# Linear attention into a channel mix on one core: k in uneven runs of tokens into a ring of squares, r and v on token tiles, and a new order

## The chip, the core and the metric

The kernel runs on one core of a Trainium2 chip. The metric is device time in microseconds of one execution, the median of several. Its engines are TensorE (PE, whose weight loads are listed as PEld), VectorE (DVE), ScalarE (ACT), GpSimd (POOL) and SyncE (SP). SP, ACT and POOL also issue DMAs, each into a queue of its own; the loads that convert float32 to bfloat16 on the way are issued by POOL.

## The reference

Eight batches of eight heads, 576 tokens, head width 64: a linear attention whose output (512 wide per token) goes through a channel mix.

```python
def _attn_ref(q, k, v):                       # each (8, 8, 576, 64)
    q_s = softmax(q, axis=-1)                 # over the head width
    k_s = softmax(k, axis=2)                  # over the tokens
    kv = np.einsum('bhsd,bhse->bhde', k_s, v)
    return np.einsum('bhsd,bhde->bhse', q_s, kv)

def _moe_ref(x, mu_k, mu_r, w_k, w_v, w_r):   # x (8, 576, 512)
    x_prev = tokens shifted by one, zero first
    xk = mu_k * x + (1.0 - mu_k) * x_prev
    xr = mu_r * x + (1.0 - mu_r) * x_prev
    k = np.maximum(xk @ w_k, 0.0)             # 512 -> 1024
    v = k * k @ w_v                           # 1024 -> 512
    r = 1.0 / (1.0 + np.exp(-(xr @ w_r)))
    return r * v
```

## The kernel before

Everything is bfloat16 on TensorE with float32 sums in PSUM. Every piece of work is an operation with a short name; `graph` makes the operations with what each depends on, and the long string `ORDER` gives the one sequence in which they are emitted. An engine runs its operations in that sequence. A token of `ORDER` may change the engine of an operation (`ACT!load00q1`), give it a buffer (`:0`), or make it wait for another operation (`^rrec000`).

**Attention, per batch b and half g of the heads** (names end in b, g and for the first two batches a quarter index): `load` brings q, k and v; `expq`, `expk` are exps on ACT; `rsum`, `rrec`, `scale` (DVE) make the softmax of q; `cast` (ACT) makes v bfloat16 for batches from 1 on, while batch 0's v is converted by its load into `vb`. `T` are the transposes of q (L361), `KV` the products of k and v (L391), `Z` the sums over k; from batch 2 on all of this is one block, `B` or `TKV`. `rz`, `kvn` or `w` (DVE) divide by the sums, `qt` (ACT) copies the transposed q out of PSUM, `edge` copies the column for the shift.

**Mix.** Batches 0 and 1 are fused: `wp` multiplies the small matrix by mu and 1 - mu, and `X` (L479) makes xk (m=0) or xr (m=1) directly, in two pieces of 288 tokens; `x...` (L489, L492) copies them to `xk` and `xr`, the first piece on ACT, the second on DVE. From batch 2 on, `X` (L517) makes x, `xb`/`xs` copy it (ACT), and `diff`, `sc`, `mix` (DVE) mix it with the shifted tokens.

**Channel mix.** `xk` and `xr` hold a ring of four batches (2304 tokens). The ring is cut into units of 512, 512, 512, 512 and 256 tokens, twice. In each unit, `k` (L601) makes 8 slices of 128 features from 4 matmuls each; `relu` (L588, ACT) and `sq` (L592, DVE) write the squares into one of two buffers `k_a`, `k_b` (`k2s`); for each 128 tokens of the unit `r` (L633) and `th` (ACT), then `v` (L653, 8 matmuls), `o` (L659, DVE) and two stores `st` on SP. In the first two units the k matmuls are emitted in halves, first the feature tiles of g=0 and then those of g=1.

`fill` (L292) are matmuls on a constant tile that nothing reads; 18 of them are in this order, all before the first `X`. POOL issues, in this order, batch 0's v, then batch 1's first q half, the four parts of w_k and the rest of batch 1 with w_r and w_v between:

```python
ident load00v load01v load10q0 wk11 wk00 load10q1 wk01 wk10 load11v0 load11q0 load11q1 wr ...
```

PSUM has four single banks (`mm`) and two double ones (`att`); for batch 0 an allocation `any` may use either.

Of the kernel before, what the change touches and what calls it, by code (L numbers as in the profile page):

```python
# [41 lines left out]
ORDER = """
ACT!rows ident load01q0:0 load00q0:1 ACT!load00q1 load01q1 load00v consts ACT!load00k1:2 load00k0
ACT!load01k0:3 load01v zero late fill:3 warm load10q0:4 fill.2:2 fill.3:3 wk11 fill.4:2 fill.5:3
wk00 expq000:0 wide:0 load10q1 load01k1 rsum000:0 wk01 rrec000 expq011:1 scale000:0 wk10 expq010
fill.6^rrec000:3 rsum011:1 fill.7^expq011:2 expq001 fill.8^expq010:3 rsum010 fill.9^rsum011:2
fill.31:2 rsum001 fill.10^expq001:3 expk000:0 fill.11^rsum010:2 rrec010 widecopy scale010:1
fill.12^expk000:3 expk001 fill.13:2 fill.32:2 rrec011 rrec001 KV000:0 scale001 load11v0:5 KV001
scale011 T00:1 expk011:1 Z00 expk010 fill.14:3 rz00:0 kvn00:0 fill.16:3 rest KV011:2 load11q0:6
KV010 T01:0 qt00:0 wp000:0 edge00 wp001 Z01 load11q1 qt01:1 fill.17:3 rz01:1 kvn01:1 X000:1.3  # L50
expq100:2 wp010:1 wr edge01 X001:2.0 x0000 x0001 X010:1.3 x0010 load10v0:7 k02:0 wv0 x0100 x0101
k00:1 wp011 k03:2 x0011 k01:3 load10k1:8 k00.2 k01.2 relu00:0 k02.2 load11v1 relu01:1 X011:1.0
relu02:2 load10v1 sq01:0 k03.2 x0110 x0111 k05:1 load10k0 relu03:1 sq00 expq111:0 load11k0:9 k04:3
expq101 k06:0 expq110 rsum101:2 relu04:0 k07:2 sq03 sq02 relu06:1 rsum110:3 load11k1 r03:3
cast100:0 sq04 muload wv1 r00:0 relu07:2 cast110:1 sq07 r01:2 rsum111 relu05:0 th00:0 rrec101
r02:1 rsum100 th03:1 wv2 th01:2 v010:0 rrec100 rrec111 rrec110 sq05 expk101:2 load20v0:10
scale100:2 v030:3 th02:3 load20q0:0 scale101 cast111 v000:2 cast101 scale110:0 expk100 v020:1
scale111 expk110:0 load21q0:1 TKV10:0 expk111 load20k0:2 rz10:2 kvn10:0 TKV11:1 qt10:2 wp101:0
v021 rz11:0 load21v0:3 kvn11:1 v011 sq06 qt11:0 v031 wp100 load30v0:4 v001 edge10 v012 load30q0:6
edge11 v022 o01 cast200:2 X100:0.1 load21k0:5 wp110:1 v002 x1001 x1000 v032 o00 mu:0 load31q0:7  # L60
X110:1.0 o02 load40q0:8 k13:2 x1100 expq200:1 x1101 k11:1 wp111 expq210:2 rsum200:0 k13.2 k11.2
load31k0:9 X111:1.0 relu13:2 mucopy o03 load30k0:10 expk200:1 k12:0 x1111 st03 k14:2 rrec200 x1110
st00.2 rsum210:1 load41q0:0 st00 k10:3 relu11:0 X101:0.1 st01 relu14:1 sq11:1 st03.2 cast210:0
sq13 k10.2 load31v0:1 st02.2 x1011 k12.2 relu10:0 k15:1 x1010 sq10 load40v0:2 k16:2 scale200:1
relu12:2 relu15:0 k17:3 expq300:0 rrec210 sq14 r10:0 sq12 relu17:1 rsum300:2 TKV20:1 relu16:2
cast300:1 load40k0:3 r11:1 rrec300 rz20:1 scale210:2 th10:4 r13:3 expk210:2 r12:2 w20:0 sq16
qt20:1 scale300:0 v100:0 load50q0:6 th11:5 B21:0.1 sq15 expq310:1 sq17 v120:1 rz21:2 th13:6 w21:1
rsum310:3 xs20:0 xb20 v110:3 load41k0:4 v121 qt21:0 edge20 diff20:0 load50k0:5 v111 th12:0
sc2001:0 expq400:2 rrec310 X21:1.0 sc2000 o11 r20:2 load50v0:7 xb21:1 mix200 v130:3 o12 xs21
th20:1 load41v0:8 edge21 v101 st12 diff21:1 expk300:0 st01.2 v131 sc2100:1 sc2101 expk310:1  # L70
load51q0:10 sc2010:2 TKV30:1 mix210 cast310:2 o13 k20:1 load51v0:9 scale310:1 k21:2 relu20:2
cast400:0 o10 k25:3 rz30:0 load61q0:1 sc2011 st10 k23:1 relu21:0 w30:2 sc2111:0 st12.2 qt30:2
sq20:0 st10.2 k27:0 rsum400:0 expk400:2 k22:2 sq21 load51k0:2 mix201 relu23:1 B31:0.1 relu22:2
rrec400 sc2110 relu27:0 k24:1 sq22 load60q0:3 xs30:0 rz31:1 mix211 relu25:2 k26:2 xb30 sq27 sq25
r23:0 w31:0 relu24:0 edge30 scale400:2 qt31:1 r22:3 expq410:0 diff30:0 r21:1 sq23 B40:1.0 sc3001:1
th21:2 load60v0:0 rsum410:1 relu26:2 v200:1 xs31:1 xb31 sc3000 sq26 v220:2 sq24 th22:0 edge31
mix300 th23:4 v201 expq500:1 sc3011:2 diff31:1 v221 o20 cast410:1 load60k0:6 v210:3 sc3101:0 st20
o22 expk410:0 v230:0 st20.2 load70q0:8 sc3100 sc3010 v211 mix310 expq510:2 load61k0:4 mix301 v231
expk500:1 load61v0:10 o21 k30:1 o23 st21.2 cast500:2 load71q0:5 sc3110:1 k31:2 st02 sc3111 st23
rz40:2 mix311 relu30:1 load71k0:7 k32:3 st22 expk510:2 sq30:1 st11 rrec410 k33:0 w40:1 st22.2  # L80
scale410:0 relu31:2 st13.2 load71v0:2 k34:1 relu32:0 st21 relu33:1 sq31 k35:2 qt40:0 sq32 sq33
# [737 lines left out]
```

## Time and profile before

| what | value |
|---|---|
| runs | 201.43, 201.09, 199.63 us; median 201.09 |
| profiled execution | span 199.1 us from its first to its last instruction; no time beside the span is given for it |
| granted TensorE clock | 1.00 throughout |
| PE, PEld, DVE, ACT, POOL busy | 187.2, 92.3, 150.8, 145.7, 43.6 us |
| bytes | 33.56 MB read, 9.44 MB written, DMA queues busiest up to 100 us |
| first fused mix, first k, first r | 16.17, 18.65, 26.29 us |
| last matmul, end of the span | about 195.2, 199.1 us |

Busy time of an engine is the time in which at least one of its instructions ran. Pipelined matmuls overlap, so a 128x512 matmul is shown with 379 ns although the next begins 216 ns after it. A line of the timeline gives the start, the length, the engine, the source line and the tiles; the brackets give the engine's idle time just before and what ended it.

### The profile page before, as it was taken

What the parts mean: (1) busy time and instruction counts of PE and PEld (TensorE: products, weight loads), DVE (VectorE), ACT (ScalarE), POOL (GpSimd) and SP (SyncE); (2) the same over time, 40 slices, a digit from 0 to 9 for tenths busy, and PEclk for the clock granted to TensorE, in tenths of its full rate; (3) what the DMA queues carried; (4) which work ended last, traced back from release to release, by engine and by line L of the source; (5) the groups of instructions that cost most, each with busy time, mean ns of one, the idle gap of its engine ahead of it and who ended that gap; (6) DMA issues with size and microseconds to landing.
All of it is one profiled execution on the core that took longest, in us unless ns stands there. A gap on an engine that the chain in (4) does not pass through costs nothing.

```text
span 199.1 us, 5164 instructions
## 1 busy us (share of the span) xinstructions
PE 187.2 (94%) x2059; PEld 92.3 (46%) x2085; DVE 150.8 (76%) x348; ACT 145.7 (73%) x224; POOL 43.6 (22%) x70
## 2 busy tenths in 40 slices
PE   6598999989999999999999999999999999999992
PEld 2045445434444444445565545544444544444751
DVE  1588486889989999999999995999825459732531
ACT  3377798799999999999999488777624762552340
POOL 8435438954424312622000000000000000000000
PEclk9999999999999999999999999999999999999999
DMA  6999999999999998799942130422044013402513
GB/s 199 256 276 281 279 336 230 367 397 393 415 393 395 400 407 328 243 412 405 376 116 54 45 90 0 102 63 54 3 105 107 0 23 85 105 2 53 121 40 105
DMA packets 16544, 40.13 MB, mean 202 GB/s; under 512 B 2300, under 2 KB 5640, under 8 KB 16520
## 3 DMA queue, kind: packets, MB, share of 16 engines
q0 software_dynamic: 9440, 27.99, 42.3%
q1 hardware_dynamic: 6400, 10.65, 19.5%
q10 hardware_dynamic: 680, 1.15, 1.6%
q8 instruction: 16, 0.26, 0.6%
q14 instruction: 8, 0.07, 0.1%
HBM read 33.56 MB, written 9.44 MB: 216 GB/s over the span
## 4 chain that ended last, share of the span: by engine, by line
PE 50%; issue 1%; ACT 0%; DVE 0%
PE mm_c L653 7%; PE mm_d L653 6%; PE mm_d L601 5%; PE mm_c L601 4%; PE mm_a L653 4%; PE mm_b L601 4%; PE mm_a L601 4%; PE mm_b L633 3%; PE mm_b L653 3%; PE mm_a L633 3%; PE mm_d L633 2%; PE mm_c L633 1%; PE att_b L517 1%; PE att_a L517 1%; PE att_a L391 1%
## 5 line engine op out<-in xcount | busy, mean ns | idle before, releaser
L653 PEld LDWEIGHTS <-k_a 128*128 128x128 bf16 x144 | 13.8, 98 | 16.9 <-DVE k_a L592 0.6
L633 PEld LDWEIGHTS <-xr 128*128 128x128 bf16 x144 | 13.9, 98 | 16.4 <-issue 0.2
L653 PEld LDWEIGHTS <-k_b 128*128 128x128 bf16 x152 | 14.3, 98 | 15.0 <-issue 0.6
L633 PE MATMUL mm_b<-wr,xr 128*128 128x512 bf16 x45 | 12.2, 379 | 0.2
L601 PEld LDWEIGHTS <-wk_bb 128*128 128x128 bf16 x80 | 7.8, 98 | 7.7
L601 PEld LDWEIGHTS <-wk_ba 128*128 128x128 bf16 x80 | 7.7, 98 | 7.8 <-issue 0.3
L601 PEld LDWEIGHTS <-wk_ab 128*128 128x128 bf16 x80 | 7.6, 98 | 8.0 <-DVE xk L489 0.5
L601 PEld LDWEIGHTS <-wk_aa 128*128 128x128 bf16 x80 | 7.4, 98 | 8.3 <-issue 1.0
L633 PE MATMUL mm_a<-wr,xr 128*128 128x512 bf16 x39 | 10.2, 379 | 0.1
L588 ACT ACTIVATE rel_a<-mm_b 128x512 bf16<-128x512 f32 (+1 forms) x10 | 5.8, 576 | 5.9 <-PE mm_b L601 5.9
L588 ACT ACTIVATE rel_c<-mm_c 128x512 bf16<-128x512 f32 (+1 forms) x11 | 6.6, 598 | 1.2 <-PE mm_c L601 1.2
L633 PE MATMUL mm_c<-wr,xr 128*128 128x512 bf16 x28 | 7.2, 379 | 0.0
L592 DVE TENSOR_TENSOR k_b<-rel_a 128x512 bf16<-128x512 bf16 (+1 forms) x13 | 5.2, 401 | 2.4 <-ACT rel_a L588 2.0
L633 PE MATMUL mm_d<-wr,xr 128*128 128x512 bf16 x27 | 7.0, 379 | 0.0
L592 DVE TENSOR_TENSOR k_a<-rel_c 128x512 bf16<-128x512 bf16 (+1 forms) x14 | 5.7, 404 | 1.6 <-ACT rel_c L588 1.5
L592 DVE TENSOR_TENSOR k_b<-rel_c 128x512 bf16<-128x512 bf16 (+1 forms) x14 | 5.4, 387 | 1.8 <-ACT rel_c L588 1.4
L292 PE MATMUL mm_d<-still 128*128 128x512 bf16 x8 | 4.7, 592 | 2.1 <-DVE still L233 1.9
L592 DVE TENSOR_TENSOR k_a<-rel_b 128x512 bf16<-128x512 bf16 (+1 forms) x12 | 4.9, 404 | 2.4 <-ACT rel_b L588 2.4
L588 ACT ACTIVATE rel_c<-mm_b 128x512 bf16<-128x512 f32 (+1 forms) x6 | 3.5, 578 | 4.3 <-PE mm_b L601 4.3
L292 PE MATMUL mm_c<-still 128*128 128x512 bf16 x8 | 4.5, 611 | 2.2 <-ACT eq_b L326 2.2
L601 PE MATMUL mm_c<-xk,wk_ab 128*128 128x512 bf16 (+1 forms) x22 | 6.1, 361 | 0.3 <-DVE xk L489 0.2
L592 DVE TENSOR_TENSOR k_a<-rel_a 128x512 bf16<-128x512 bf16 (+1 forms) x14 | 5.4, 388 | 1.2 <-ACT rel_a L588 1.1
(358 smaller groups left out, 555.2 us busy)
## 6 DMA issues: line engine op xcount, KB each, us to landing
out_dram<-th_a SPq DMA_DIRECT2D x13, 128.0 KB, 4.6
out_dram<-th_b SPq DMA_DIRECT2D x12, 128.0 KB, 4.0
out_dram<-th_c SPq DMA_DIRECT2D x10, 128.0 KB, 2.8
out_dram<-th_d SPq DMA_DIRECT2D x10, 128.0 KB, 2.4
out_dram<-th_e SPq DMA_DIRECT2D x10, 128.0 KB, 3.9
raw_k<-in_v_dram POOLq DMA_DIRECT2D x2, 576.0 KB, 6.9
raw_a<-in_q_dram POOLq DMA_DIRECT2D x2, 576.0 KB, 10.0
raw_b<-in_q_dram POOLq DMA_DIRECT2D x2, 576.0 KB, 9.9
```

The source lines that it names most:

```text
L292: return kn.nc.tensor.matmul(kn.bank(slot), lhsT=kn.still[:, 0:128], rhs=kn.still[:], start=True, stop=True)
L391: kn.nc.tensor.matmul(kn.half(slot, r)[two[u], KVO:KVO + n], lhsT=kn.eks[ek.index][two[r], j, u, :], rhs=by, start=(j == 0), stop=(j == J ...
L517: kn.nc.tensor.matmul(kn.half(slot, u)[two[r], to:to + n], lhsT=kn.ws[w.index][two[u], r, :], rhs=kn.qts[qt.index][two[u], r, 64 + at:64 + ...
L588: kn.nc.scalar.activation(out=kn.rels[rel.index][:, 0:n], in_=kn.bank(kf)[:, 0:n], func=ACT.Relu, scale=HALF_ROOT)
L592: kn.nc.vector.tensor_tensor(out=kn.k2s[k2.index][:, fc, 0:n], in0=kn.rels[rel.index][:, 0:n], in1=kn.rels[rel.index][:, 0:n], op=ALU.mult)
L601: kn.nc.tensor.matmul(kn.bank(kf)[:, 0:n], lhsT=kn.wk[fc // 4][ct % 2][:, ct // 2, (fc % 4) * 128: (fc % 4) * 128 + 128], rhs=kn.xs[0][:, ...
L633: kn.nc.tensor.matmul(kn.bank(rps), lhsT=kn.xs[1][:, ct, c:c + 128], rhs=kn.wr[:, ct, :], start=(ct == 0), stop=(ct == CT - 1))
L653: kn.nc.tensor.matmul(kn.bank(vps)[:, 0:width], lhsT=kn.k2s[k2.index][:, ft, 128 * m:128 * m + 128], rhs=wv_of(ft)[:, part], start=(ft == ...
```

## The change

- **k in uneven runs.** The first half of the ring's work is cut into runs of 256, 320, 448, 512, 512 and 256 tokens, the second into 256, 512, 512, 512, 512. A run of 256 tokens puts two feature slices into one bank and evicts them together. The first three runs are emitted in halves.
- **A ring of squares.** `k2` is one buffer of 1024 tokens; a square waits for the v of the tile 1024 tokens earlier.
- **r and v on tiles of their own.** 36 tiles of 128 tokens, no longer tied to the units of k; `mixes` gives each the pieces of the mix that its tokens need, so a first run can begin with the first 288 tokens of a batch.
- **Copies split.** `qt` of batches 0 and 1 is two copies, one on ACT and one on DVE. `X` is one operation for each 288 tokens, and for batch 0, m=0, both engines copy one half of each piece. `wp` for m=1 is on POOL for batch 0 too. Batch 1's `cast` is on POOL.
- **Batch 1** has `T` and `KV` of its own instead of `TKV`, and may use the `mm` banks.
- **Loads.** Batch 0's v on POOL waits for `expq000`. SP issues the two small mu loads, then q00 first half, both of q01, and two k halves; ACT issues q00's second half first, and the two other k halves after three exps. wk00 and wk01 come ahead of wk10 and wk11.
- **Order.** `ORDER` is new throughout; it has 9 fillers.

```diff
-UNITS = ((0, 512), (512, 512), (1024, 512), (1536, 512), (2048, 256))
+K2 = 1024
+UNITS = (((0, 256), (256, 320), (576, 448), (1024, 512), (1536, 512), (2048, 256)),
+         ((0, 256), (256, 512), (768, 512), (1280, 512), (1792, 512)))
+TILES = RING // 128
-EARLY_UNITS = 2
+EARLY_UNITS = 3
 ORDER = """
-ACT!rows ident load01q0:0 load00q0:1 ACT!load00q1 load01q1 load00v consts ACT!load00k1:2 load00k0
-ACT!load01k0:3 load01v zero late fill:3 warm load10q0:4 fill.2:2 fill.3:3 wk11 fill.4:2 fill.5:3
-wk00 expq000:0 wide:0 load10q1 load01k1 rsum000:0 wk01 rrec000 expq011:1 scale000:0 wk10 expq010
...
+ident ACT!load00q1:0 zero SP!muload ACT!rows consts load00q0 warm load01q0:1 load01q1 fill:0
+fill.2:1 fill.3:2 fill.4:3 load00k0:2 load01k1:3 expq001:0 wide:0 rsum001:0 expq000
+load00v^expq000 rsum000 expq010:1 ACT!load00k1 load01v rsum010:1 ACT!load01k0 load10q0:4 rrec010
+rrec000 scale000:0 wk00 expk000:0 scale010:1 load10q1 widecopy wk01 expq011 late rrec001 mu:1
+scale001 fill.5^rrec001:2 load11q1:5 fill.6^expq011:3 wk10 rsum011 expk001 fill.7^scale001:0
+expk011:1 rest Z00:0 T00 fill.8^expk011:2 qt000:0 qt001 expk010 rrec011 rz00:0 wk11 KV000 scale011
+KV001 Z01:1 edge00 T01 rz01:1 kvn00:0 fill.9^rz01:3 mucopy wp000:0 wp001 qt011:1 X0000:3 KV011
+load11v0:6 expq100:2 x0000b KV010 X0001:0 kvn01:1 x0000a X0010:2 x0001b wp011:1 x0010 wp010 k0_2:2
+k0_0:3 rsum100:2 qt010 load11q0 x0001a load11k1:7 edge01 rrec100 X0100:2 X0110:1 wr x0100a x0100b
+X0101:0 k0_0.2 load10k0:8 x0101a x0101b k1_0:0 scale100:2 expq101 k0_2.2 wv0 k0_1 k0_3 rsum101
...
-        def cast_v(u):
-            kn.nc.scalar.copy(
+        def cast_v(op, u):
+            copy = kn.nc.scalar.copy if op[0].engine == "ACT" else kn.nc.gpsimd.tensor_copy
...
-        def copy_qt(slot):
+        def copy_qt(slot, r=None):
             to = kn.qts[qt.index]
-            if kn.whole(slot) is not None:
+            if r is not None:
+                copy = kn.nc.vector.tensor_copy if r else kn.nc.scalar.copy
+                return copy(out=to[:, r, 64:64 + S], in_=turned(slot, r))
...
+            def mixed_x(m, t, slot):
+                for i in range(2):
+                    for r in range(2):
+                        for u in range(2):
...
+    def mixes(half, c, n, g, m):
+
+        made = []
+        for b in range(c // S, (c + n - 1) // S + 1):
+            parts = mixed[4 * half + b, g, m]
+            for t, part in enumerate(parts):
+                if len(parts) == 1 or (c < b * S + 288 * t + 288 and c + n > b * S + 288 * t):
+                    made += part
+        return made
...
     def unit(half, c0, n, index):
         early = index < EARLY_UNITS
+        at = (RING * half + c0) % K2
+        pair = n == 256
...
+            def square():
+                src = kn.rels[rel.index][:, 0:width]
+                to = kn.k2[:, fc, at:at + n]
+                if pair:
+                    src = src.rearrange("p (f c) -> p f c", f=2)
+                    to = kn.k2[:, fc:fc + 2, at:at + n]
+                kn.nc.vector.tensor_tensor(out=to, in0=src, in1=src, op=ALU.mult)
...
+        for fc in range(FT):
+            kf, lo = (kfs[fc // 2], 256 * (fc % 2)) if pair else (kfs[fc], 0)
+            mm = kdone[-1] if pair and fc % 2 else None
+            for cts in ((0, 2), (1, 3)) if early and not (pair and fc % 2) else ((0, 2, 1, 3),):
...
+    def tile_out(half, m):
+        index = TILES * half + m
+        c = 128 * m
...
+        at = 128 * index % K2
...
-    kn.k2s = buffers("k2", [128, FT, 512], BF16)
+    kn.k2 = const.tile([128, FT, K2], BF16, name="k2")
```

448 lines of the change are left out of this document (226 added, 222 removed).

## The prediction

> **What bounds the kernel now.** I read the page first (busy shares, then the chain), then busy time by stretches, then the timeline of the first 64 us engine by engine, then the DMA issues. The busy shares and the chain:
>
> ```profile
> PE 187.2 (94%) x2059; PEld 92.3 (46%) x2085; DVE 150.8 (76%) x348; ACT 145.7 (73%) x224; POOL 43.6 (22%) x70
> ...
> PE 50%; issue 1%; ACT 0%; DVE 0%
> ```
>
> TensorE sets the end. The chain can be followed back to 93.48 us, and from there to 195.2 it is matmul after matmul. So the time is the start-up, plus the matmuls, plus TensorE's gaps, plus a tail. The stretches (columns: PE, PEld, DVE, ACT, POOL busy, granted clock, DMA share, GB/s) show where something else is close behind:
>
> ```profile
> 14.00:18.65 4.65, 3.60 (x141) 2.74 (x135) 3.70 (x17) 4.34 (x8) 3.08 (x5) 1.00 1.21 244
> 18.65:26.29 7.64, 7.59 (x51) 3.43 (x49) 4.84 (x12) 5.60 (x11) 3.29 (x7) 1.00 1.17 282
> 26.29:63.89 37.60, 36.46 (x497) 17.61 (x501) 33.04 (x71) 35.71 (x53) 20.07 (x30) 1.00 1.03 370
> 63.89:93.48 29.59, 29.15 (x365) 14.01 (x362) 29.19 (x61) 29.07 (x41) 9.39 (x13) 1.00 0.97 367
> 93.48:199.00 105.52, 100.52 (x951) 51.22 (x962) 72.85 (x165) 64.39 (x104) 0.72 (x1) 1.00 0.31 82
> ```
>
> From 26 to 93 us VectorE and ScalarE are nearly as full as TensorE; after 93 they have slack. Little can be won after 18.65, where k starts: TensorE idles only about 2 us between there and 93.48. What can be won lies ahead of it. TensorE's own timeline (start, length, tile; in brackets the idle time before and what ended it):
>
> ```profile
> 11.73 0.63 PE L292 MATMUL mm_d<-still 128*128 128x512 bf16 x1
> ...
> 14.38 0.38 PE L292 MATMUL mm_d<-still 128*128 128x512 bf16 x1 [0.16 <-issue]
> ...
> 16.17 0.44 PE L479 MATMUL att_b<-qt_a,wp_a 64*64 64x288 bf16 x8 [0.25 <-DVE rz_b L402]
> ...
> 18.04 0.44 PE L479 MATMUL att_b<-qt_b,wp_b 64*64 64x288 bf16 x8 [0.64 <-ACT xk L489]
> ...
> 18.65 0.39 PE L601 MATMUL mm_a<-xk,wk_aa 128*128 128x512 bf16 x1
> ...
> 26.29 0.81 PE L633 MATMUL mm_d<-wr,xr 128*128 128x512 bf16 x3
> ...
> 63.89 0.39 PE L601 MATMUL mm_b<-xk,wk_aa 128*128 128x512 bf16 x1
> ```
>
> L292 are filler matmuls; the first matmul of batch 0's mix starts at 16.17, k at 18.65, r at 26.29. What that waits for is data (ACT, then POOL, then the DMA issues with median us to landing):
>
> ```profile
> 8.31 1.26 ACT L326 ACTIVATE eq_b<-raw_a 128x576 bf16<-128x576 f32 x2 [3.12 <-DMA raw_a<-in_q_dram]
> ...
> 13.19 1.26 ACT L326 ACTIVATE ek_b<-raw_d 128x576 bf16<-128x576 f32 x2 [0.62 <-DMA raw_d<-in_k_dram]
> ```
> ```profile
> raw_b<-in_q_dram SPq DMA_DIRECT2D x1, 288.0 KB, 3.3
> ...
> raw_c<-in_k_dram ACTq DMA_DIRECT2D x1, 288.0 KB, 8.6
> ...
> vb_a<-in_v_dram POOLq DMA_DIRECT2D x1, 288.0 KB, 9.4
> ...
> raw_k<-in_v_dram POOLq DMA_DIRECT2D x2, 576.0 KB, 6.9
> ```
>
> One early q half lands in 3.3 us; those beside v and weights take 8.6. The last k half is there at 13.2.
>
> **The start, walked through.** POOL issues nothing until `expq000` is done; SP carries five of batch 0's q and k halves behind the two small mu loads, ACT one q half first and two k halves after three exps. ScalarE's table load (1.28 us) now follows three DMA issues and not five, so `warm` ends at about 3.5. `expq001`, `expq000`, `expq010` (0.6 each) then end at 4.15, 4.75 and 5.35, if their loads land 3.3 us after issue. ACT issues two k halves (0.45 each) until 6.2; they land at 3.3 us, 8.6 and 9.1. VectorE runs from 4.2: three rsum (2.05), two rrec (0.3), two scale (1.35), constants (0.25), rrec, scale, rsum, rest (1.85): 10.0. The transposes wait for the z matmuls (k half at 8.6, exp to 9.2), so `qt001` runs 10.15 to 10.8; then rrec, rz, scale, edge, rz (1.3 with one wait): 12.3; kvn, mucopy, wp: 13.1. `X0000` starts at about 13.2, against 16.17. This needs v at 11.2: POOL's issue at 4.75 plus 6.4, the shortest v row (one of the two `raw_k` loads); the other end is 9.4.
>
> From `X0000` to k proper: VectorE has `x0000b`, `kvn01`, `x0001b`, `wp010`, `rsum100`, `edge01` (0.37, 0.3, 0.37, 0.41, 0.67, 0.1) and ScalarE `x0000a`, `x0010`, `qt010` (0.3, 0.71, 0.57) with waits: 16.4. `X0100` and its copy (0.25 + 0.45) bring k at 17.3; its first matmuls with the g=0 halves run before. wk00 and wk01 are POOL's fourth and sixth load; the POOL queue moves 146 to 194 packets per us when alone (stretches 12 to 16), which puts them at about 13.2 and 15.2.
>
> k for 576 tokens is 32 x 9/8 x 0.216 = 7.78, less 0.44 already done, plus two X (0.5) and `T10` (0.31): 8.15, and 0.4 for banks that wait for a relu: r at 25.9. By r the kernel before had 512 tokens done and no `T10`; to be level it would stand at 26.29 + 0.86 + 0.31 = 27.46. **Gain 1.55.** wr, queued on POOL behind `wp001` and `wp011`, is issued at 16.7 and lands at 23 to 26 (row: 9.6): in time, or 0.4 late.
>
> **The other parts.** (a) The mu transpose and its copy move to the start. Before they cost TensorE 0.15 at 39.13 and a wait of 0.38 at 42.98 (released by DVE mu). Gain 0.5; I take 0.35. (b) Uneven runs: the 256-column k matmuls in the old tail go four in 0.44 us, 512 columns four in 0.86, so 32 more matmuls with the same columns cost nothing on TensorE; evictions fall from 80 to 76, since 256-column runs share a bank in pairs. (c) Batch 1's four v casts leave ScalarE (0.57 each) for POOL. No row shows a POOL cast; by ScalarE's row it takes 0.57, by POOL's 128x128 multiply (0.45) times 4.5 it takes 2.0; I take 1.3, from the 128x128 select (0.29). Behind the first stand `load10k1`, wv1, wv2; behind the last `load21v0`, `load20k0` and `wp111`. At 1.3 the last ends near 33, when `KV10` wants it; at 2.0 it is 2 us late, and `v3_1` and those behind it in TensorE's order wait. (d) Four q copies split: ScalarE loses 4 x 0.45, VectorE gains 4 x 0.67 = 2.7. Two wp go to POOL: VectorE -0.8. (e) Up to `mix210`, which the k run at 1024 waits for in both, VectorE also has `scale310` more (1.27): together about +2.6 of work, against idle time of 2.8 + 4.6 in the second and third stretch. My count from KV to `mix210` is 25.5 of VectorE against 26.6 of TensorE: covered, by 1 us. If that cover is gone, k at 1024 waits, and the lead goes.
>
> In the tail the last two halves of v and the last stores keep their form: 0.
>
> **Sum.** 1.55 + 0.35 = 1.9 off a span of 199.1: 197.2. The page gives no time around the span; the runs' median, 201.09, lies 2.0 above it (the lowest, 199.63, 0.5). Against the median: **199.2**.
>
> **Rivals.** *VectorE takes the bound before 64 us.* For: its 88% there, 2.6 more work, and the POOL casts: the one VectorE square that ran beside POOL's multiply (35.39) took 0.61 instead of 0.42. Against: the idle time above. Price: 4 x 1.3 us of casts at 0.19 per 0.89 is 1.1, plus the uncovered half of the 2.6: 2.4, so 201.6. The Trainium skill (SBUF — State Buffer, the single rule on the shared port pair) says that a VectorE operation with two SBUF inputs and a GpSimd one that reads SBUF block each other wholly; that row agrees in kind, and by the rule up to all 5.2 us of casts could be lost.
>
> *TensorE is not at full rate when k starts.* There are 9 fillers in place of 18. At 11.73 a filler of 512 columns still takes 0.63, at 14.38 it takes 0.38; work had been dense since 9.05, so it took between 2.7 and 5.3 us of density. In my walk TensorE is dense from 8.4 to 15.8, with fillers between small matmuls: enough. If it isn't, k runs its first 2.7 to 5.3 us at half rate and loses 1.4 to 2.7: about 201.2. The Trainium skill (TensorE: Matmul & The Clock Gate, Part 1) has the clock released after some 3.4 us of sustained activity and gated again after as long an idle window; by it the loss would be 1.7.
>
> *The late halves stay late.* For: two k halves wait on ACT behind three exps, v on POOL behind one; at the rows of before (8.6) the k halves issued at 5.3 and 5.8 land at 13.9 and 14.4. Then `expk001`, z, `T00`, `qt001`, `scale011`, `expk010`, `Z01` and `kvn00` follow one another, and `X0000` starts at 18.3: 5.1 later than walked, so 204.3. It decides from 1.9 us of lateness on. Against: the 8.6 were measured with three queues moving; here POOL's first bytes come about 3.6 us after its issue (1.44 to 5.0 before), thus after 8.
>
> *More than forecast*: ScalarE's relief of 4 us brings the exps forward, and the other 1.5 us of TensorE's gaps up to 64 go too: 197.4.
>
> **How the numbers follow.** Forecast 0.42 (198.2 to 200.3), VectorE 0.15, clock 0.10, late halves 0.19, more 0.14. One per cent (2 us) is about what can be told from no change. Faster by more: all of the last and 0.19 of the forecast, 0.33; slower: the late halves, 0.19; within: the rest, 0.48. Range 196.8 to 203.3: it holds all but the late halves and the best of the gains.
>
> **What would show it.** First L601 with TensorE dense at 17 to 18 us, not 18.65; r near 26 with 576 tokens done; fillers gone and 512 columns at 0.216 apart by then; the last batch-0 k exp ended before 12; no TensorE idle over 0.5 us ahead of the k run at 1024, which starts near 62. Wrong if `X0000` comes after 15, if POOL's casts pass 2 us each, or if VectorE has no idle time between 30 and 62 and TensorE waits on a mix.

## The result, and the profile after

The changed kernel takes 209.16 us (median of four runs: 208.55, 209.64, 208.68, 210.13) against 201.26 us for the kernel before, run on the same chip: a ratio of 1.042, with a 95% interval of 1.036 to 1.048 (the quotient of the two medians is 1.039, inside the interval). Faster had been forecast, 199.2. The profiled execution took 208.55 us with a span of 206.8, so 1.75 lie around the span (the forecast had 2.0). Some executions of th_free, before_queues and all_b below were disturbed and slower: their times and ratios leave these out, but the profiles of th_free and all_b are of such an execution.

The busy shares and the shares of the chain that ended last, from the page of the changed kernel:

```profile
PE 189.7 (92%) x2108; PEld 95.2 (46%) x2108; DVE 152.4 (74%) x343; ACT 141.7 (69%) x218; POOL 46.5 (22%) x76
...
PE 78%; DMA 9%; ACT 5%; DVE 4%; issue 1%; SPq 1%; DVEq 0%; ACTq 0%
```

TensorE has at most 2.5 us more to show for itself (in the kernel before, 26 matmuls fewer are on record than weight loads, so its 187.2 is a little short), and the span is 7.7 longer: most of the loss is idle time. The chain can now be followed back to the start, and 9% of it are transfers. The stretches between the same landmarks as before (columns: PE, PEld, DVE, ACT, POOL busy, granted clock, DMA share, GB/s):

```profile
17.65:22.77 5.12, 4.48 (x89) 2.93 (x89) 3.97 (x11) 2.34 (x6) 4.16 (x9) 1.00 0.88 180
22.77:31.79 9.02, 8.98 (x95) 6.22 (x95) 7.09 (x18) 7.63 (x16) 5.77 (x10) 1.00 1.02 205
31.79:70.13 38.34, 35.64 (x485) 16.97 (x483) 31.60 (x66) 29.29 (x46) 18.68 (x28) 1.00 1.05 382
70.13:102.00 31.87, 31.45 (x301) 15.36 (x301) 29.70 (x61) 28.73 (x41) 8.03 (x12) 1.00 0.89 285
102.00:207.00 105.00, 99.69 (x1025) 49.79 (x1022) 71.14 (x158) 65.23 (x99) 2.81 (x4) 0.99 0.34 88
```

The landmarks themselves are in TensorE's timeline: batch 0's first KV, the first mix, its second pair of heads, dense k, the first r, the k run at 1024, and a block of the second half.

```profile
15.01 0.99 PE L399 MATMUL att_a<-vb_a,ek_a 64*64 64x64 bf16 x36 [0.82 <-DVE rz_a L406]
17.65 0.45 PE L496 MATMUL mm_c<-qt_a,wp_a 64*64 64x288 bf16 x1
21.73 0.28 PE L496 MATMUL mm_a<-qt_b,wp_b 64*64 64x288 bf16 x1 [0.64 <-DVE rsum_c L346]
22.77 0.38 PE L647 MATMUL mm_d<-xk,wk_ab 128*128 128x256 bf16 x2
31.79 0.38 PE L680 MATMUL mm_b<-wr,xr 128*128 128x512 bf16 x1
70.13 0.59 PE L647 MATMUL mm_c<-xk,wk_aa 128*128 128x512 bf16 x2 [1.96 <-ACT th_f L685]
114.34 0.22 PE L542 MATMUL att_b<-qt_c,w_c 64*64 64x64 bf16 x4 [0.83 <-ACT qt_c L377]
```

Against the kernel before, the loss splits in three:

| stretch | before | to be level | after | lost |
|---|---|---|---|---|
| start to first r | 26.29 | 27.46 (64 tokens more of k and one T done by then) | 31.79 | 4.3 |
| first r to the k run at 1024 | 37.60 | 36.43 (that work less) | 38.34 | 1.9 |
| k run at 1024 to the end | 135.2 | 135.2 | 136.7 | 1.5 |

**The start**, in the chain of waits (start, length, what):

```profile
1.89 4.53 DMA raw_b<-in_q_dram
...
6.44 5.54 DMA raw_c<-in_k_dram
...
12.01 0.69 ACT ek_a L331
...
12.74 0.40 PE att_a L386 x18
13.14 0.52 PE att_a L366 x18
...
13.69 0.65 ACT qt_a L375
...
14.36 0.46 DVE qt_a L375
...
14.93 0.04 DVE rz_a L406
...
15.01 0.99 PE att_a L399 x26
```

The q half that `expq010` needs lands at 6.42; only behind that exp does ScalarE issue the late k halves, and the first lands at 11.98. Then everything stands in a row: exp, z, the transposes behind z, ScalarE's copy, VectorE's copy behind ScalarE's, `rz00` behind that, and KV, which writes the PSUM slot that all of these read.

**The k run at 1024** stands behind a store:

```profile
60.61 0.59 DVE th_f L706
...
61.39 0.31 SPq L716
...
61.74 7.63 DMA out_dram<-th_f
...
69.48 0.60 ACT th_f L685
```

`th7` writes the buffer of `th6` (`th7:5`, `th6:5`); tile 6's store is issued at 61.4 and lands 7.6 us later, ScalarE waits for it, and TensorE for ScalarE's bank. Three of the seven `th` buffers hold tiles 0, 1 and 3, whose `o` were done by 45; but `st0`, `st1` and `st3` come later in SP's order, so only four buffers go round.

### The profile page after: what moved, and what is told of

Same layout as the page of the kernel before. It is cut to its first block, busy times and chain, and to the rows that moved or that the text cites. A ratio compares the mean times of both kernels' runs of the same rounds, so it can differ in the third digit from the quotient of the medians.

```text
span 206.8 us, 5191 instructions
## 1 busy us (share of the span) xinstructions
PE 189.7 (92%) x2108; PEld 95.2 (46%) x2108; DVE 152.4 (74%) x343; ACT 141.7 (69%) x218; POOL 46.5 (22%) x76
## 4 chain that ended last, share of the span: by engine, by line
PE 78%; DMA 9%; ACT 5%; DVE 4%; issue 1%; SPq 1%; DVEq 0%; ACTq 0%
PE mm_d L647 8%; PE mm_a L700 8%; PE mm_a L647 7%; PE mm_b L700 7%; PE mm_d L700 6%; PE mm_b L647 6%; PE mm_c L680 6%; PE mm_c L647 6%; PE mm_c L700 5%; DMA out_dram<-th_f 4%; PE mm_a L680 3%; DMA raw_c<-in_k_dram 3%; PE mm_d L680 3%; DMA raw_b<-in_q_dram 2%; PE mm_b L680 2%; PE att_b L399 2%
## 5 line engine op out<-in xcount | busy, mean ns | idle before, releaser
L700 PEld LDWEIGHTS <-k 128*128 128x128 bf16 x296 | 28.2, 98 | 31.6 <-issue 0.7
L636 DVE TENSOR_TENSOR k<-rel_c 128x512 bf16<-128x512 bf16 (+2 forms) x31 | 13.0, 421 | 8.3 <-ACT rel_c L626 8.2
L680 PE MATMUL mm_c<-wr,xr 128*128 128x512 bf16 x60 | 15.4, 379 | 0.1
L636 DVE TENSOR_TENSOR k<-rel_a 128x512 bf16<-128x512 bf16 (+2 forms) x23 | 9.3, 403 | 4.0 <-ACT rel_a L626 4.0
L700 PE MATMUL mm_a<-wv_a,k 128*128 128x512 bf16 (+1 forms) x44 | 10.9, 370 | 0.0
L700 PE MATMUL mm_b<-wv_a,k 128*128 128x512 bf16 x40 | 10.3, 379 | 0.0
L636 DVE TENSOR_TENSOR k<-rel_b 128x512 bf16<-128x512 bf16 (+2 forms) x22 | 8.8, 401 | 1.7 <-ACT rel_b L626 1.7
L700 PE MATMUL mm_d<-wv_a,k 128*128 128x512 bf16 x36 | 9.2, 379 | 0.0
L647 PE MATMUL mm_d<-xk,wk_ba 128*128 128x512 bf16 (+2 forms) x30 | 7.9, 345 | 0.1
L647 PE MATMUL mm_d<-xk,wk_bb 128*128 128x512 bf16 (+2 forms) x30 | 7.9, 345 | 0.0
```

The lines of the kernel that those rows point to most:

```text
L636: kn.nc.vector.tensor_tensor(out=to, in0=src, in1=src, op=ALU.mult)
L647: kn.nc.tensor.matmul(kn.bank(kf)[:, lo:lo + n], lhsT=kn.wk[fc // 4][ct % 2][:, ct // 2, (fc % 4) * 128: (fc % 4) * 128 + 128], rhs=kn.xs[ ...
L680: kn.nc.tensor.matmul(kn.bank(rps), lhsT=kn.xs[1][:, ct, c:c + 128], rhs=kn.wr[:, ct, :], start=(ct == 0), stop=(ct == CT - 1))
L700: kn.nc.tensor.matmul(kn.bank(vps)[:, 0:width], lhsT=kn.k2[:, ft, at:at + 128], rhs=wv_of(ft)[:, part], start=(ft == 0), stop=(ft == FT - 1))
```

## The experiments

Each run gives the median and the ratio to the kernel before on the same chip with its 95% interval; the changed kernel stands at 1.042 [1.036, 1.048].

### First round: one part at a time

**k_early**: the k halves ahead of the exps.

```diff
-ident ACT!load00q1:0 zero SP!muload ACT!rows consts load00q0
+ident ACT!load00q1:0 zero SP!muload ACT!rows ACT!load00k1:2 ACT!load01k0:3 consts load00q0
```

> The two k halves that ScalarE's queue issues behind three exps are issued ahead of the exps instead; all else as in the changed kernel. Theory A (the late halves set the start): they are there before 9, expk001 starts near 9.5 instead of 12.01, X0000 near 15.2 instead of 17.65, the first r matmul near 29.5 instead of 31.8; the time falls by 2 to 2.5, to about 206.7. Rival B (v, which lands at 13.2, and the chain of copies behind the transposes set it): X0000 not before 16.8, and the time falls by less than 1. Rival C (the same bytes, only shared otherwise): the q halves land about 1 us later, expq010 ends later, and nothing is gained.

Measured: 208.99 us, 1.036 [1.030, 1.043]. `expq010` starts at 7.93 instead of 6.43, `expk001` at 11.88 instead of 12.01, X0000 at 17.92. What k's issue gains q loses, as in rival C.

**v_early**: `load00v` and `load01v` first on POOL, not held.

> Batch 0's two v loads go out first on POOL's queue, not held for expq000. Theory A (k's late halves set the start): v lands about 4 us earlier and nobody waits for it; X0000 stays at 17.65 within 0.3, or comes up to 1.5 later because v's bytes move beside q's and k's; time 209 to 210.5. Rival B (v's landing sets KV000): KV000 and X0000 come 1 to 2 us earlier, time 207 to 208.

Measured: 211.42 us, 1.049 [1.043, 1.056]. `expk001` starts at 14.92, X0000 at 20.57. v's bytes move ahead of k's and q's, and X0000 comes 2.9 later, where theory A had allowed 1.5. Rival B, by which KV and X0000 come earlier with v, is not borne out either.

**psum_apart** and **kv_free**: slots of their own for T00 and KV00; in kv_free `rz00` also goes ahead of `qt001`.

```diff
-            qtp = kvp = Slot("any")
+            kvp = Slot("any")
+            qtp = Slot("any") if (b, g) == (0, 0) else kvp
...
-rest Z00:0 T00 fill.8^expk011:2 qt000:0 qt001 expk010 rrec011 rz00:0 wk11 KV000
+rest mucopy Z00:0 T00:1 fill.8^expk011:2 rz00:0 qt000:0 qt001 expk010 rrec011 wk11 KV000
```

> Batch 0's first pair of heads gets separate PSUM slots for its transposes and for KV and Z (as in the kernel before), so that KV000 doesn't wait for qt000, qt001 and rz00 to read the shared slot; mucopy moves a little ahead because the third slot lies on its bank. Theory A (k's late halves): KV000 moves up by 0.8, to 14.2, but its reader rz00 stays behind qt001 in VectorE's order: X0000 comes 0.3 to 0.8 earlier, time 208.3 to 208.9. Rival D (the shared slot is the main loss of the start): X0000 comes 1.5 or more earlier, time under 207.7.

> As psum_apart, and rz00, the only reader that KV000 then still waits for, runs on VectorE ahead of qt001 and rrec011 and not behind them. Theory D (KV000 waits for copies that have nothing to do with it; separate slots alone didn't take the wait away, since rz00 stood behind qt001): KV000 starts within 0.6 of the end of T00, not 1.35 after it, or at v's landing if that is later, and the distance from the landing of the last k half (expk001's start) to X0000 falls from 5.65 to about 4.5; the time falls by about 1, to 207.5 to 208.2. Rival: v's landing holds KV000 (13.2 in the changed kernel's profile), or X0000 waits for qt001 and the edge copy then: the distance stays above 5.2.

Measured: 207.74 us, 1.031 [1.026, 1.036], and 207.64 us, 1.033 [1.027, 1.040]. In psum_apart KV000 still waits for `rz00` behind `qt001`, and from `expk001` to X0000 it takes 5.70 against 5.64 in the changed kernel: its profile doesn't show where its lower time comes from. In kv_free KV000 starts 0.47 after T00's end (13.99 to 14.46), but X0000 doesn't move (17.66): T01 stands ahead of it in TensorE's order and waits for `scale011`, which VectorE does behind the copies. The distance from `expk001` to X0000 is 5.3, 0.3 less than in the changed kernel: the shared slot alone is not what makes the start long.

**th_free**: tile 3's stores as soon as it is done, and its buffer for `th7`.

```diff
-load21k0:6 o3 load31q0:7 o1 ... mix200 th7:5 load40k0:10 ... r12:2 st3 o10 xs31 st3.2
+load21k0:6 o3 st3 st3.2 load31q0:7 o1 ... mix200 th7:2 load40k0:10 ... r12:2 o10 xs31
```

> Tile 3's two stores are issued as soon as tile 3 is done (they stood ten tiles later in SyncE's order), and th7 writes tile 3's buffer instead of th6's; the start is untouched. Theory E (the store of tile 6 holds th7, th7 holds ScalarE, and TensorE loses its 1.96 us before the k run at 1024 to it): that wait is gone, the k run at 1024 starts near 68 instead of 69.9, and the time falls by 1.5 to 2, to about 207.3. Rival F (VectorE's mix210, done at 67.4, or ScalarE's queue of work would have held it anyway): the wait is named otherwise, under 0.7 is won, time 208.5 to 209.2.

Measured: 205.46 us; 1.018 [1.012, 1.023]. From r to the k run at 1024 it takes 36.70 instead of 38.34, with no wait ahead of it in TensorE's timeline:

```profile
70.18 0.59 PE L700 MATMUL mm_d<-wv_c,k 128*128 128x512 bf16 x2
70.61 0.59 PE L647 MATMUL mm_c<-xk,wk_aa 128*128 128x512 bf16 x2
```

Theory E is borne out: the wait is gone and the stretch is 1.6 shorter. Between the medians it is 3.7; what the other 2 are is not explained.

**more_fill**: three more fillers ahead of Z00 and KV000.

> Three more filler matmuls in TensorE's idle time ahead of Z00 and KV000; all else as in the changed kernel. Theory G (TensorE comes to X0000 at half rate and loses there what the forecast gave to that rival): X0000's eight matmuls take 0.44 in all and not 0.88, KV010's and KV011's 0.4 instead of 0.88, the distance from X0000 to dense k falls from 5.1 to about 4.2, time 208.2 or less. Rival H (that stretch waits for VectorE's and ScalarE's copies, whatever TensorE's rate): the matmuls are shorter, the distance stays within 0.3, time 209 to 209.5.

Measured: 208.57 us, 1.038 [1.033, 1.043]. KV000 still took 0.99 and X0000's matmuls 0.45: the fillers did not bring full rate, so the run decides nothing between G and H.

**pair_first** and **all_a**: the loads, exps and sums of the first pair of heads first; all_a adds the repairs so far and puts X0000 ahead of the second pair's work.

```diff
-ACT!rows consts load00q0 warm load01q0:1 load01q1 ... load00k0:2 load01k1:3
+ACT!rows ACT!load00k1:2 consts load00q0 load00k0 warm load01q0:1 load01q1 ... load01k1:3
```

> The loads of batch 0's first pair of heads (both q and both k halves) go ahead of those of the second pair on SyncE's and ScalarE's queues, and the exps, sums and scalings follow in that order; v stays held for expq000. Theory I (the start moves at the rate at which the bytes come in, some 280 per ns, so what counts is whose bytes come first): expk001 starts near 8.5 instead of 12.01, Z00 and T00 near 9.5; then v, landing at about 13, is what KV000 waits for, X0000 starts at 15.3 to 16; the second pair's halves land at 12 to 13, X0100 about as now, so dense k comes 0.5 to 1.5 earlier, time 207.6 to 208.6. Rival A (it is the queue behind ScalarE's exps alone, not the rate): the half of k that stays behind the exps comes at 12 as before, and the second pair's chain moves dense k later by 1 or more, time over 209.5.

> Together: the first pair's loads first, with its v not held; separate PSUM slots for its transposes and KV, rz00 ahead of qt001; KV000 and X0000 ahead of the second pair's z and transposes; two fillers more; tile 3's stores early and th7 in tile 3's buffer. If theories D, E and I add up: X0000 near 13.5 to 14.5, dense k near 20, the first r matmul near 29, no wait at the k run at 1024, span 202 to 203.5, time 204 to 205.5: still 2 to 4 above the kernel before. If the start's gains are lost again to the second pair: X0000 early, dense k at 22 to 23, time 206.5 to 207.5 as with the free buffer alone.

Measured: 207.74 us, 1.035 [1.028, 1.041], and 207.67 us, 1.033 [1.029, 1.038]. In pair_first KV000 starts at 11.71 and X0000 at 16.89, but the second pair's last k half lands at 14.42 and dense k starts at 22.28, 0.5 earlier. In all_a X0000 starts at 15.14 and the first r at 33.45. In pair_first, what the first pair wins the second loses for the most part; all_a does not show it as cleanly, since the granted clock read 0.50 in its profile from 18 to 24 us.

The stretch from the first r to the k run at 1024 can be compared across all kernels. In those with the old order of stores (the changed kernel, k_early, v_early, psum_apart, kv_free, more_fill, pair_first and, further below, hold_rest) it takes 37.4 to 38.9, each time with `th_f` behind its store. In the six with tile 3's stores early and `wp` as it was (th_free, all_a, chain_th, chain2_th, all_b, fill_full) it takes 36.4 to 36.7, and 35.3 in wp_apart, all_c and mu_later, each time without that wait. One kernel stands between: chain, below, without the edit, also took 36.71. There the store landed sooner (from its chain of waits):

```profile
63.25 5.35 DMA out_dram<-th_f
```

ScalarE still waited 0.99 for it, TensorE no more. So the wait depends on how soon the store lands, 5.35 or 7.63; the edit takes away what the landing can cost.

### Second round: the chain behind the loads

**chain** and **chain_th** (with th_free's edit): transposes ahead of z, KV ahead of z, slots apart for both pairs, the second pair's sums and copies ahead of `rz00`, twelve fillers in place of nine; loads and holds as in the changed kernel.

```diff
-expk011:1 rest Z00:0 T00 fill.8^expk011:2 qt000:0 qt001 expk010 rrec011 rz00:0 wk11 KV000 scale011
-KV001 Z01:1 edge00 T01 rz01:1 kvn00:0 fill.9^rz01:3 mucopy wp000:0 wp001 qt011:1 X0000:3 KV011
+T00:1 fill.9^scale001:2 fill.10^rsum011:3 qt000:0 rrec011 scale011 mucopy rest expk001 expk011:1 expk010 wk11
+T01:3 fill.11^scale011:0 qt001 edge00 fill.12:1 KV000:0 KV001 Z00 KV011:2 KV010 Z01
+rz00:0 kvn00:0 wp000:0 wp001 qt010:1 X0000:1 rz01:1 kvn01:1 qt011 wp011:1 wp010 x0000b edge01
```

> The loads' queues and holds stay as in the changed kernel; only what follows them is put in another order: separate PSUM slots for transposes and KV of both pairs, each pair's transposes as soon as its q is scaled (not behind z, which waits for the last k half), KV ahead of z, the second pair's sums and scaling and both q copies ahead of rz00, second-pair work ahead of X0000 where its data is there, and seven fillers in place of five in the same stretch. Theory J (the loss of the start lies in the order of the chain behind the last k half, 8.5 from the last exp of k to dense k against 4.9 in the kernel before, and not in the loads): dense k starts 4 to 5 after the last exp of k, at 18 to 19 where it was 22.8; the first r matmul near 28; span about 203, time 204.5 to 206. Rival I (the bytes come too late whatever follows): dense k not before 21, time over 208.

> The order of the run named chain, and tile 3's stores early with th7 in tile 3's buffer. By theories J and E together: dense k at 18 to 19, no wait at the k run at 1024, time 202 to 204, level with or up to 1.5% above the kernel before; what is left is the second half. Without J: as with the free buffer alone, 206 to 207.

Measured: 206.60 us, 1.028 [1.021, 1.036], and 204.80 us, 1.021 [1.013, 1.028]. From the start of the last exp of k to dense k (the first matmul with `wk_ab`) it takes 8.55 in the changed kernel, 8.57 in k_early and 8.47 in v_early, whatever the loads; 6.39 in chain_th, where dense k starts at 20.8 and not at 18 to 19. This does not yet show theory J, for the order is not all that differs. KV000 took 0.66 in chain_th, the length it has in the kernel before (`12.99 0.66` in TensorE's timeline), and 0.99 in the changed kernel: the rate differs too. The kernels below all have the new order, with further edits. There dense k starts at 20.4 to 20.8 where KV000 takes 0.66, and at 21.3 to 22.4 where it takes 0.99:

| kernel | KV000 | last exp of k | dense k | distance |
|---|---|---|---|---|
| changed kernel (old order) | 0.99 | 14.22 | 22.77 | 8.55 |
| chain2_th | 0.99 | 12.99 | 21.29 | 8.30 |
| wp_apart | 0.99 | 14.16 | 22.23 | 8.07 |
| all_b | 0.99 | 15.05 | 22.38 | 7.33 |
| chain_th | 0.66 | 14.43 | 20.82 | 6.39 |
| fill_full | 0.66 | 14.70 | 20.45 | 5.75 |
| all_c | 0.66 | 14.61 | 20.70 | 6.09 |
| mu_later | 0.66 | 13.26 | 20.61 | 7.35 |

What the order is worth by itself stays open: at half rate dense k comes 0.4 to 1.5 earlier than in the changed kernel, and th_free (old order), chain_th and chain2_th can't be told apart by their times (1.018, 1.021 and 1.018). The run named chain had the granted clock at half for 6 us of its profiled start (the last three columns are the clock, the DMA share and GB/s):

```profile
20.00:22.00 2.00, 2.00 (x27) 0.96 (x25) 0.83 (x3) 0.77 (x3) 2.00 (x4) 0.50 0.93 294
```

Its execution with the clock at 1.00 throughout took 205.05.

**before_queues**: the kernel before, with two k halves behind three exps and v held.

> The kernel before, with the changed kernel's handling of two things: ScalarE issues its two k halves behind three exps, and POOL's v (and all behind it) is held for the first exp of q. Rival A (the late loads are what costs): X000 3 or more later than 16.2, time over 203.5. Theory J: the bytes are shared otherwise, X000 0 to 1.5 later, time 201 to 202.5.

Measured: 201.79 us, 1.004 [0.9998, 1.008]. In its profile X000 started at 14.57, 1.6 earlier than before. In the old order the new queues cost less than 1%: that the late loads by themselves are the cost (rival A) does not hold there.

### Third round: what was left

**hold_rest**: batch 1's q and w_k held for `expk000`.

> The changed kernel with one thing more held: POOL's loads behind v (batch 1's q halves, w_k) wait for the first exp of k, so that between 7 and 9 only batch 0's own q, k and v move. Theory K (they share the DMA engines with what POOL prefetches; with all of batch 0 in 16 us at some 250 GB/s the landing is set by what else moves): the two late k halves land by about 10.5 instead of 12.0, expk001 and X0000 come 1 to 1.5 earlier, time 207.5 to 208.3. Rival (a half issued at 6.4 simply takes 5.5, whatever moves beside it): landing at 11.7 to 12.5, time 209 or, since w_k comes later, more.

Measured: 208.81 us, 1.036 [1.032, 1.040], and `expk001` started at 13.55, later than before. Theory K is not borne out. In twelve kernels with the same loads ahead of it, this exp starts between 11.06 and 13.88, and `expq010` between 5.93 and 7.20. So 13.55 here, or 11.88 in k_early, is not yet an effect of the edit; `expq010` at 7.93 in k_early and `expk001` at 14.92 in v_early lie outside the spread.

**chain2_th**: chain_th, with slots of two tiles for all that two engines copy by halves. **all_b**: also `r17` ahead of the block that waits 0.83.

```diff
-T00:1 ... T01:3 ... KV000:0 ... KV011:2 ... X0000:1 ... X0001:0 ... X0010:2
+T00:3 ... T01:2 ... KV000:0 ... KV011:1 ... X0000:3 ... X0001:2 ... X0010:0
```

> The run named chain_th, with the PSUM slots of batch 0 dealt out otherwise: what ScalarE and VectorE copy half each (both transposes, X0000, X0001, X0100) lies in slots made of two banks that are two tiles, KV and Z in the slots that are one tile; the second pair's two q copies go ahead of rz00. Theory L (two engines that read one PSUM tile do so one after the other: qt001 started when qt000 ended, x0000a when x0000b ended): the two copies of each pair now run side by side, TensorE's wait of 1.51 before the first k falls under 0.7, dense k at 18.5 to 19.2 instead of 20.3, first r matmul about 1.2 earlier than in chain_th against the same last exp, time 203 to 204. Rival: VectorE's chain rz, kvn, wp of both pairs sets it and the copies don't matter: under 0.4 won, time 204.5 to 205.

> The run named chain2_th, and one r tile of the second half (r17) ahead of the block that waits 0.83 for a q copy. Theory: that wait is gone and nothing takes its place: 0.5 to 0.8 less than chain2_th, time 202.3 to 203.3, so still 0.5 to 1 per cent above the kernel before. Rival: the wait goes to the next instruction, no change.

Measured: 205.13 us, 1.018 [1.013, 1.023], and 204.57 us, 1.014 [1.009, 1.019]. The copies do run side by side now. ScalarE's and VectorE's timelines, first of the changed kernel, then of chain2_th:

```profile
13.69 0.64 ACT L375 COPY qt_a<-att_a 128x576 bf16<-128x576 bf16 x1 [0.42 <-PE att_a L366]
...
14.36 0.46 DVE L375 COPY qt_a<-att_a 128x576 bf16<-128x576 bf16 x1 [2.57 <-ACT qt_a L375]
```
```profile
11.28 0.64 ACT L376 COPY qt_a<-mm_c 128x576 bf16<-128x576 bf16 x1 [1.83 <-PE mm_d L367]
...
11.31 0.46 DVE L376 COPY qt_a<-mm_d 128x576 bf16<-128x576 bf16 x1 [0.37 <-PE mm_d L367]
```

The mechanism of theory L is shown, its gain is not: this execution ran its start at half rate. In all_b the wait of 0.83 went to the next block (1.70 at 116.84): its rival.

**fill_full**: chain2_th with seven more fillers, so that TensorE is dense from 7 us on.

```diff
-fill.5^expk000:2 fill.6:3 mu:1
+fill.13^expq010:2 fill.14:3 fill.15:2 fill.16:3 fill.5^expk000:2 fill.6:3 fill.17:2 mu:1
```

> The run named chain2_th with seven more filler matmuls between 7 and 13 us, in TensorE's idle time, so that it is dense from 7 on. Theory G (half rate at the start costs the part that the forecast's rival named): full rate by KV000 (0.66 instead of 0.99), X0000's eight in 0.44 in all, dense k 1 to 1.7 earlier against the same last exp, time 203.4 to 204.1. Rival H (VectorE's chain sets it): the matmuls are shorter and TensorE waits instead, under 0.4 won, 204.7 to 205.2.

Measured: 203.81 us, 1.014 [1.010, 1.017]. TensorE's timeline in chain2_th, then in fill_full:

```profile
14.35 0.99 PE L400 MATMUL att_a<-vb_a,ek_a 64*64 64x64 bf16 x36
...
16.85 0.45 PE L498 MATMUL mm_c<-qt_a,wp_a 64*64 64x288 bf16 x1
```
```profile
14.84 0.66 PE L400 MATMUL att_a<-vb_a,ek_a 64*64 64x64 bf16 x36
...
16.72 0.31 PE L498 MATMUL mm_c<-qt_a,wp_a 64*64 64x288 bf16 x1
```

From the last exp of k to dense k it is 5.75 now, against 8.30 in chain2_th, and dense k starts 0.8 earlier although the last exp of k comes 1.7 later. That is theory G, worth 1.3 between the medians and 0.9 by the ratios, whose intervals overlap; the lengths of the matmuls decide.

**wp_apart**: chain2_th, with batch 0's `wp` on VectorE again and batch 1's on POOL held until VectorE's are done. **all_c**: fill_full and wp_apart together. **mu_later**: all_c with the two small mu loads behind SP's five halves.

```diff
-                me.append(add("POOL" if m else "DVE", ...
+                me.append(add("POOL" if m and b else "DVE", ...
...
-edge11 wp100:1 v1_1 wp110:0 wp111 v0_2 ... x1101 wp101
+edge11 wp110:0 v1_1 wp100:1 wp111^wp110 v0_2 ... x1101 wp101^wp100
```

> The run named chain2_th, with batch 0's wp001 and wp011 back on VectorE (behind wp010 and x0000b, X0010 later on TensorE) and batch 1's two POOL multiplies held until VectorE's are done, wp110 ahead of wp100; so no wp of the two engines runs beside another. Theory M (they slow one another): each VectorE pair takes 0.49 again, TensorE's wait ahead of batch 1's first X (0.98 in chain2_th) falls to under 0.4, POOL's weight and batch 1 loads are issued 2 to 4 earlier, time 203.6 to 204.4. Rival: POOL's multiplies come later and their own X waits, no gain.

> The run named chain2_th with both: seven more fillers, and the multiplies taken apart. If G and M add up: span 200.5 to 201.8, time 202.3 to 203.6, within 0.5 to 1 per cent of the kernel before; if the data (last exp of k at 14 to 15) sets the start, time 204 or more.

> The run named all_c, with the two small mu loads behind SyncE's five q and k halves instead of ahead of them, and the mu transpose on TensorE after the second pair's transposes. Theory N (the two issues push all halves back by 0.74): the exp of the second pair's first q half starts near 6.2 instead of 6.9, the last exp of k 0.7 earlier than 14.6, time 201.7 to 202.3. Rival (the rate of bytes sets the last landing, or v does, which KV000 waits for until 14.2): last exp within 0.4 of 14.6, time 202.4 to 203.

Measured: 203.90 us, 1.014 [1.011, 1.017]; 202.71 us, 1.010 [1.006, 1.013]; 203.34 us, 1.012 [1.007, 1.016]. VectorE's and POOL's `wp` in the changed kernel and in all_c:

```profile
17.27 0.75 DVE L485 TENSOR_TENSOR wp_a<-kvn_a,mu_wide 128x128 bf16<-128x128 f32 x2
17.40 0.94 POOL L485 TENSOR_TENSOR wp_a<-kvn_a,mu_wide 128x128 bf16<-128x128 f32 x2 [3.52 <-DVE mu L290]
...
40.24 0.95 POOL L485 TENSOR_TENSOR wp_a<-kvn_a,mu_wide 128x128 bf16<-128x128 f32 x2
40.29 1.09 DVE L485 TENSOR_TENSOR wp_b<-kvn_b,mu_wide 128x128 bf16<-128x128 f32 x2
```
```profile
15.74 0.49 DVE L487 TENSOR_TENSOR wp_a<-kvn_a,mu_wide 128x128 bf16<-128x128 f32 x2
...
38.24 0.48 DVE L487 TENSOR_TENSOR wp_a<-kvn_a,mu_wide 128x128 bf16<-128x128 f32 x2
38.64 0.48 DVE L487 TENSOR_TENSOR wp_b<-kvn_b,mu_wide 128x128 bf16<-128x128 f32 x2
38.86 0.58 POOL L487 TENSOR_TENSOR wp_a<-kvn_a,mu_wide 128x128 bf16<-128x128 f32 x1 [0.60 <-DVE wp_a L487]
```

Theory M is borne out: VectorE's pairs are back at 0.49 and 0.48, and TensorE's wait ahead of batch 1's X, 0.98 in chain2_th and still there in fill_full, is gone in wp_apart and all_c. Fill_full's wait:

```profile
39.93 0.32 PE L498 MATMUL att_b<-qt_b,wp_a 64*64 64x288 bf16 x4 [0.69 <-DVE wp_a L487]
```

From r to the k run at 1024 wp_apart takes 35.32, against 36.71 in chain2_th. Between the medians it is 1.2, and with G it adds up: 2.4 of 2.5. From r to the k run at 1024 all_c takes 35.32, 1.1 less than the 36.43 that would be level with the kernel before. So all_c, with these repairs, ends 1.8 us of span above the kernel before: 2.3 in the start, 0.6 at the end, less that 1.1. No version beat the kernel before. In mu_later the last exp of k comes about 1.3 earlier than in all_c, at 13.26, and `expq010` at 5.88; but chain2_th, with the mu loads still ahead, has 12.99 and 5.93, so one profile doesn't show that theory N has the landing right. KV000 starts at 14.08 against 14.20, and nothing is won: the chain of waits goes through TensorE's fillers, T00, VectorE's scaling of the second pair (12.20 to 12.97) and T01. In all_c it does not go through the last exp of k either.

## Why the prediction was wrong, step by step

The forecast's span was 197.2; the profiled one is 206.8. Its own landmarks split the 9.6: X0000 at 13.2 against 17.65 (4.45), from there to dense k 4.1 against 5.12 (1.0), from dense k to r 8.6 against 9.02 (0.4), from r to the k run at 1024 about 36.1 against 38.34 (2.25), and the rest (1.5). The prediction's own sign of being wrong, X0000 after 15, came true.

- **"If their loads land 3.3 us after issue" failed.** The k halves were to land at 8.6 and 9.1. The issue came about 1.1 later (6.44 and 6.84 instead of 5.35 and 5.8), since `expq010` waited for its half until 6.42, and the first landing took 5.5. That is 3.4 of the 4.45 at X0000 (12.0 instead of 8.6). The term was a latency where it should have been a rate: the eight q and k halves are 2.36 MB, and by 9.1 they ask for 332 GB/s from 2 us on with nothing else moving. The DMAs moved:

```profile
2.00:7.00 5.00, 3.15 (x5) 0.65 (x3) 1.51 (x2) 3.41 (x5) 1.44 (x2) 1.00 0.98 322
7.00:12.00 5.00, 1.70 (x4) 0.41 (x4) 4.53 (x15) 1.86 (x4) 3.94 (x7) 1.00 1.04 229
12.00:17.00 5.00, 3.27 (x109) 2.45 (x109) 1.59 (x7) 3.16 (x5) 0.72 (x1) 1.00 1.16 299
```

  that is 2.75 MB by 12 us, 275 GB/s; at that rate the halves alone need until 10.6. k_early, v_early and pair_first agree: an earlier half makes another later. The Trainium skill (DMA: Bandwidth & Descriptors, the section that issuing engines are not separate DMA queues) says that the queues of SP, ACT and POOL share the same 16 engines; these runs agree. What sets 12 rather than 10.6 is not shown. By 12 the queues of SP and ScalarE had moved 2.24 MB, and what shares with k is POOL's queue: from 7 to 12 its transfers took 69% of the DMA engines' time for 0.52 MB, ScalarE's 27% for 0.48. In hold_rest, with batch 1's prefetches held, POOL's still took 68% for 0.50 MB; so v's halves are the likely ones, but no run held v until k had landed.
- **The walk behind the k half was mis-sized.** The walk had the transposes wait for z, the q copies follow the transposes and KV follow v; it did not see that T and KV share one PSUM slot, so that KV waits for `qt000`, `qt001` and `rz00`. From the exp of k to X0000 it took 5.64 where the walk had 4.6, which is the other 1.05 of the 4.45, and up to dense k 1.0 more. The slot is not the whole of it: with slots apart kv_free still takes 5.3. From the last exp of k to dense k the changed kernel takes 8.55; with the new order it is 7.3 to 8.3 at half rate and 5.75 to 7.35 at full rate, so a part of the 8.55 belongs to the next term. That the two copies follow one another is part of it: the Trainium skill (PSUM — Partial Sum Buffer, PSUM bank collisions raise a hardware error) says that two engines' accesses to the same quadrant (32 partitions) of one bank collide, and that accesses to different banks run clean. The halves lie in two banks, but of one tile, and the wait is between tiles; in chain2_th, with two tiles, they overlap.
- **The clock rival (0.10) came true in part, on top of the others.** "TensorE is dense from 8.4 to 15.8, with fillers between small matmuls: enough" failed: TensorE was busy 4.1 of the 8 us from 8 to 16, and KV000 took 0.99 and X0000's matmuls 0.45, at half rate. But the rival had k itself at half rate; by 21.73 the mixes took 0.28 to 0.31 and dense k ran at full rate, so the price was paid earlier, in KV and the first mixes. Its size, 1.4 to 2.7, was near: fill_full won 1.3 (0.9 by the ratios).
- **The late halves rival (0.19)** had the landing right in kind: 13.9 forecast for the first half, 12.0 seen. The second (14.4) can't be read from this trace, where its exp stands behind other work. X0000 at 18.3 (17.65 seen) came close in part by luck, an earlier landing and a longer walk behind it; and its time of 204.3 lacked the next two terms.
- **The store was not in the forecast at all.** No step asked which `th` buffer a tile writes and when its store lands. By th_free it is worth 1.6 us in its stretch.
- **"Two wp go to POOL: VectorE -0.8" had the wrong sign.** VectorE's four pairs took 0.75, 0.72, 1.09 and 0.74 beside POOL's, where six pairs took 0.48 or 0.49 before, when POOL's two ran at another time: it saves 0.98 and loses 1.34, and TensorE waits 0.74 at 41.89 for the second. I had the Trainium skill's rule for this (SBUF — State Buffer, the single rule) at hand and put it on the casts, not on `wp`; these pairs agree with it in kind. By the runs the term is the 1.2 that wp_apart wins.
- **Right:** POOL's casts are cheap (0.72, 0.68, and 1.28 for two, against 1.3 each); uneven runs cost TensorE nothing (all_c is 1.1 ahead between r and the k run at 1024); the mu transpose no longer stops TensorE; wr was issued 5 late (21.78, behind `wp001`) and still in time; VectorE did not take the bound: `mix210` ended at 67.4, before the k run could start.
- **The tail, put at 0, took part of the last 1.5.** The last matmul of the kernel before, of the changed kernel and of all_c:

```profile
194.77 0.38 PE L653 MATMUL mm_b<-wv_c,k_b 128*128 128x256 bf16 x2
```
```profile
202.14 0.38 PE L700 MATMUL mm_c<-wv_c,k 128*128 128x256 bf16 x2
```
```profile
195.96 0.38 PE L703 MATMUL mm_c<-wv_c,k 128*128 128x256 bf16 x2
```

  From the k run at 1024 to its end it is 131.26, 132.39 and 131.29; behind it the span goes on for 3.95, 4.28 and 4.56. So of the 1.5, 1.1 lie ahead of the last matmul and 0.3 behind it; all_c has the 1.1 back, and its 0.6 is the longer tail alone. The wait of 0.83 at 114.34 is not the cause, for all_c has it too, at 108.16. Why the tail is longer was not looked into.
- **Two sums don't come out as written.** (d) and (e) make 2.7 - 0.8 + 1.27 = 3.2 of VectorE's work and not 2.6. And the rows have TensorE idle for 1.2 us from 18.65 to 63.89, so the rival "more than forecast" had no other 1.5 to win there; 199.2 less 1.5 would be 197.7. Neither decided the outcome.

## What to carry to other kernels

Size the start of a kernel by bytes and rate first; a landing time taken from one early transfer need not hold for eight that are issued together. Where a change deals out buffers by hand, walk each one to the transfer or the reader that frees it: a store behind busy loads, or a copy by another engine, is a wait that no dependency in the code names. And compare the same stretch across all runs before a change in it is put down to an edit: with equal loads one exp moved by 2.8 us here, and the rate of TensorE changed the distance that the order was to shorten.

## What was not expected of the hardware

- A store of 128 KB took 7.6 us to land while the DMAs moved 383 GB/s (60 to 70 us), and the two slowest buffers' stores 5.7 and 6.2 in the median; in the kernel before the medians were 2.3 to 4.6.
- TensorE stayed at half rate through some 7 us of small matmuls in chain2_th: it was busy 7.86 of the 8 us from 13 to 21, KV000 took 0.99 at 14.35 and dense k, at 21.29, ran at full rate, while the granted clock read 1.00. So half rate is read from the matmuls' lengths, not from that column. Whether it is the size of the matmuls or the phase was not tried; the Trainium skill (TensorE: Matmul & The Clock Gate, Part 1) has the rate released after some 3.4 us of sustained activity, which this stretch doesn't show.
- In two profiled executions the granted clock itself fell to 0.50 as the work became dense: in chain from 20 to 24 us (0.72 in the 2 us before, 0.57 in the 2 us behind), in all_a from 18 to 24.
